# Chunk attention and a mixture of experts on one core: the values' copy behind the next scores, narrower first products, and other orders at the joints

## The chip, the cores and the metric

The kernel runs on one core of a Trainium2 chip, in one launch. The metric is the device time of that core in microseconds (us); the median of several runs is given. The engines are TensorE (PE for matmuls, PEld for their weight loads), VectorE (DVE), ScalarE (ACT), GpSimd (POOL) and SyncE (SP), from whose queue all transfers are issued. PSUM is the memory that TensorE writes its results to; a bank of it holds 128 x 512 float32 numbers.

## The reference

Attention within chunks of 64 tokens, then a mixture of four experts over all 4608 tokens (model width 512, hidden width 1024), all in float32:

```python
scores = scale * q_c @ k_c.T            # 8 batches x 8 heads, chunks of 64 x 64
attn = softmax(scores)
x = (attn @ v_c)                        # then reshaped to (4608, 512)
p = domain_probs / (domain_probs.sum(-1) + 1e-9)
for e in range(4):
    out += p[:, e] * (relu(x @ w1[e]) @ w2[e])
```

## The kernel before

Tokens come in tiles of 128 and in blocks of 512 (four tiles). Block 0 is worked on first and alone, the eight others in four pairs (pairs 0 to 3). A pass is one half (512 columns) of one expert's hidden layer, eight passes for each block or pair.

Every float32 factor is split in a high part (`hi`: a cast on ScalarE) and a low part (`lo`: a subtraction on VectorE or GpSimd), and a product is three matmuls per block of 128 rows (high x high, high x low, low x high; `TERMS`, `PARTS`). `product` issues them all, so nearly all matmuls of the profile have its line (L462). For pairs, the two products of a pass (tokens x w1 and hidden x w2) are done by a scheme with seven block products instead of eight: steps `p1` to `p7` of a group. `g` and `h` are the two groups of the first product, `a` and `b` those of the second; `WOVEN` is the order in which a later pass weaves its `g`, `h` with the `a`, `b` of the pass before. `FIRST` is the order of the first later pass (pair 1, pass 0), which has none before it, and `ALONE` that of the last product, which has none behind. The sums and parts that these steps need (`t1` to `t4` of the tokens in `Tokens`, of the hidden values in `Scaled`) are issued at numbered steps (`add(at, i, ...)`, `put(i, ...)`): the code's order is each engine's order, since the schedule is written by hand (`tc.manual_schedule()`).

Attention for a pair runs beside the passes before, tile by tile: `a_scores` (32 records of small matmuls), `a_softmax`, `a_weights`, `a_transpose`, `a_values`. All of them share the two PSUM banks `psa`: scores lie in the first half of each bank (`blocks(0)`), values in the second (`blocks(1)`). Waits are set by bank: an instruction that touches a bank waits for the other engines' earlier instructions on it. `a_next` issues a tile's values, the copy of the values to SBUF (L176), and then the next tile's scores (L140).

The start does the four tiles of block 0: loads on SP in the order of `load_all`, scores, softmax, transposes, values (`start_...`), then the products x w1 of tiles 0 and 1 together (`plain_hidden`, 256 columns), the output products of tile 0 and 1 (`o[0].whole()`, `o[1].whole()`), and tiles 2 and 3. `keep_warm` issues bf16 matmuls on zeros. A joint is the place where the last pass of a pair goes over into the first of the next: the next pair's tokens are split there (`Tokens`).

Of the kernel before, what the change touches and what calls it, by code (L numbers as in the profile page):

```python
# [8 lines left out]
F32 = mybir.dt.float32  # L9
# [15 lines left out]
WAITS = {"loads": 10, "softmax": 14, "copy": 3}  # L25
# [5 lines left out]
def chunk_attention_moe(ctx: ExitStack, tc: tile.TileContext, qk, v, v0, dp, w1, w2, out):  # L31
# [64 lines left out]
    def transpose_probs():  # L96
        flat = by_e[0].rearrange("p e t -> p (e t)")
        for i in range(0, p_rows, P):
            n = min(P, p_rows - i)
            ps = bank()[:n, :P]  # L100
            rows = hpool.tile([P, P], F32, name="s3")[:n]
# [62 lines left out]
    def a_values(t):  # L164

        s = st.pop(t)
        av = blocks(1)
        for j, rows, c, half, odd in quarters():
            nc.tensor.matmul(  # L169
                av[half, c, j], lhsT=s["v"][rows, 2 * j + odd], rhs=s["pt"][rows, j, half],  # L170
                start=True, stop=True,
            )
# [3 lines left out]
        nc.scalar.copy(  # L176
            out=xraw[pair][:, :, i * P : (i + 1) * P].rearrange("p j (c q) -> p c j q", c=2), in_=av
        )
# [407 lines left out]
    class Scaled:  # L586
# [20 lines left out]
        def __init__(self, n):  # L607
            e = n % n_pass // 2
            self.pb = [(pb[0][:, 0], pb[1])[e % 2], pb[0][:, 1]]
            self.parts, self.values = {}, {}  # L610
# [38 lines left out]
    class LaterGroup(Group):  # L649
        def __init__(self, g, left, h, apart):  # L650
            super().__init__(g, left)
            self.h = h
            i = 1 - g if apart else 0
            self.names = (f"A{i}", f"B{i}", f"C{i}", f"B{i}", "s2")
# [157 lines left out]
    def start_v(t):  # L812
        nc.sync.dma_start(out=v0s[t // GT], in_=v0[:, t : t + GT])

    def start_scores(t):

        sc[t] = bank(("A0", "A1", "C0", "C1")[t]).rearrange("p (h s) -> p h s", s=C)
        for h in range(2 * HG):
            for c in range(2):
                rows = slice(c * C, (c + 1) * C)  # L820
                nc.tensor.matmul(
                    sc[t][rows, h],
                    lhsT=qk0[t][rows, h // HG, 0, h % HG],
                    rhs=qk0[t][rows, h // HG, 1, h % HG],
                    start=True, stop=True,
                )

    def start_transpose(t):

        w = bank(("B0", "B0", "B1", "B0")[t]).rearrange("p (j s) -> p j s", s=P)  # L830
        for j in range(HG):
            nc.tensor.transpose(
                w[:, j], es[t][:, 2 * j : 2 * j + 2].rearrange("p h s -> p (h s)"), ident
            )
        pt[t] = hpool.tile([P, HG, P], F32, name=("s2", "s4")[t % 2])
        nc.scalar.copy(out=pt[t], in_=w)

    def start_values(t):
        av[t] = bank(("B1", "A0", "A1", "B1")[t]).rearrange("p (j s) -> p j s", s=P)
        for j in range(HG):  # L840
            for c in range(2):
                for half in range(2):
                    rows = slice(half * C, (half + 1) * C)
                    cols = slice(c * C, (c + 1) * C)
                    nc.tensor.matmul(
                        av[t][rows, j, cols], lhsT=v0s[t // GT][rows, t % GT, c, j], rhs=pt[t][rows, j, cols],
                        start=True, stop=True,
                    )

    def start_x(t):  # L850
        x_parts(av[t], slice(t * P, (t + 1) * P))
# [6 lines left out]
    idle = bank("C1")  # L858
# [8 lines left out]
    def load_all():  # L867
        start_load(0, 1)
        start_load(1, 2)
        start_v(0)  # L870
        w_loads(0, 0)
        start_load(2, 2)
        start_load(3, 2)
        start_v(2)
        nc.sync.dma_start(out=pr, in_=dp)
# [3 lines left out]
    def start_softmax(t):  # L879
        less_max(sc[t])  # L880
        a_exp(sc[t])

    def start_weights(t):
        es[t] = att.tile([P, 2 * HG, C], F32, name=("e", "pt")[t % 2])
        a_norm(es[t], sc[t], psa[:, 1, t * 2 * HG : (t + 1) * 2 * HG])

    def startup(beside):
# [5 lines left out]
        start_scores(0)  # L893
        start_scores(1)
        keep_warm(WAITS["softmax"])
        start_softmax(0)
        start_softmax(1)
        start_weights(0)
        for f, k in QUADS[:3]:
            w1_split(f, k, nc.gpsimd)  # L900
        start_transpose(0)
        keep_warm(WAITS["copy"])
        start_weights(1)
        start_values(0)
# [12 lines left out]
        start_softmax(3)  # L917
        start_weights(2)
        plain_hidden(0, first, order=RHS_LO_LAST, name="B0")
        w2_split(0, 1)  # L920
        plain_hidden(1, first, order=RHS_LO_LAST, name="B1")
        w2_split(1, 0)
        plain_hidden(2, first, order=RHS_LO_LAST, name="A0")
        start_weights(3)
        start_transpose(2)
        w2_split(1, 1)
        plain_hidden(3, first, order=RHS_LO_LAST, name="C0")
        start_values(2)
        start_x(2)
        norm_probs()  # L930
        o = tiles(0, 0, range(NT), ("A0", "C0", None, None))
# [3 lines left out]
        start_x(3)  # L935
# [3 lines left out]
        for f in range(NK):  # L939
            plain_hidden(f, [2, 3], alloc=False)  # L940
# [167 lines left out]
    def probs_load(n, s):  # L1108
        if not pb:
            pb.append(wpool.tile([P, PAIR, SUB], F32, name="ws"))  # L1110
            pb.append(hpool.tile([P, SUB], F32, name="s4"))
        e = n % n_pass // 2
        t = pb[1] if s == 0 and e % 2 else pb[0][:, s]
# [34 lines left out]
    FIRST = "g1 g2 g6 g5 h1 g7 h2 h6 g4 g3 h5 h7 h4 h3".split()  # L1148

    def first_later_pass(n, *_):  # L1150
# [9 lines left out]
        put(6, "b22", 0)  # L1160
        put(7, "b11", 1)
        put(9, "b21", 0)
        add(at, 9, lambda: sc.sum("t3", 0), lambda: sc.sum("t2", 0))
        put(11, "t2", 0)
        add(at, 11, lambda: sc.sum("t1", 0))
        put(12, "b22", 1)
        put(13, "b21", 1)
        put(13, "t1", 0)
        put(13, "t3", 0)
        add(at, 13, lambda: sc.sum("t4", 0, nc.gpsimd))  # L1170
        add(at, 13, lambda: sc.sum("t1", 1), lambda: sc.sum("t3", 1))
        for i, name in enumerate(FIRST):
# [3 lines left out]
        return (sc, left), []  # L1176

    def later_pass(n, ahead, late):
# [10 lines left out]

        for i, f in late:  # L1190
            add(at, i, f)
        second_half(at, ahead[0])
# [26 lines left out]
        if last_pass and more:  # L1219
# [10 lines left out]
            late = [  # L1230
                (0, lambda: x.hi("b22")), (0, lambda: first_load(pair + 2)), (5, lambda: x.lo("t4")),
                (8, lambda: x.lo("b22")),
# [5 lines left out]
        return (sc, left), late  # L1238

    def second_half(at, sc):  # L1240
# [3 lines left out]
        add(at, 1, lambda: sc.hi("t4", 0), lambda: sc.lo("t4", 0))  # L1244
# [3 lines left out]
        add(at, 6, lambda: sc.hi("t4", 1), lambda: sc.lo("t4", 1))  # L1248

    def last_products(ahead):  # L1250
# [5 lines left out]
        stages += [(wpool, "wraw", N_RAW)] * 3 + [(att, "e", 1), (att, "pt", 1)]  # L1256

        def plane(s, m, ps, engs):
# [4 lines left out]
            pool, name, bufs = stages.pop()  # L1263
            stage = pool.tile([P, NT, P], F32, name=name, bufs=bufs)
            for k, eng in enumerate(engs):
                part = slice(k * NT // len(engs), (k + 1) * NT // len(engs))
                eng(out=stage[:, part], in_=ps[:, part])
            t = (1 + pair * PAIR + s) * NT
            nc.sync.dma_start(
                out=out[t * P : (t + NT) * P, m * P : (m + 1) * P].rearrange("(i p) d -> p i d", p=P),  # L1270
                in_=stage,
            )

        act, dve = [nc.scalar.copy], [nc.vector.tensor_copy]
        for i, name in enumerate(ALONE):
# [3 lines left out]
            if name == "b2":  # L1279
# [8 lines left out]
        plane(0, 3, bank("A1"), act + dve)  # L1288

    with tc.manual_schedule():  # L1290
# [9 lines left out]
        ahead, late = None, []  # L1300
        for n in range(2 * n_pass, n_run):
            ahead, late = (later_pass if n > 2 * n_pass else first_later_pass)(n, ahead, late)
        last_products(ahead)
# [45 lines left out]
```

## Time and profile before

| | |
|---|---|
| runs | 1560.19 us median of 3 (1558.61 to 1560.2) |
| profiled execution | 1559.73 us, span 1557.9 us, mean granted clock 0.999 |
| TensorE busy | 1518.0 us, 97% of the span |
| DVE, ACT, POOL busy | 917.6, 572.5, 886.2 us |
| read and written | 244.39 and 68.23 MB, 201 GB/s over the span |

Start times are us from the span's start. In rows of the trace, a bracket holds the idle time of the engine before the instruction and what ended it; `A<-xh,wf` is what is written and what is read, buffer numbers left out; "x12" is a number of like instructions merged in one row.

### The profile page before, as it was taken

What the parts mean: (1) busy time and instruction counts of PE and PEld (TensorE: products, weight loads), DVE (VectorE), ACT (ScalarE), POOL (GpSimd) and SP (SyncE); (2) the same over time, 40 slices, a digit from 0 to 9 for tenths busy, and PEclk for the clock granted to TensorE, in tenths of its full rate; (3) what the DMA queues carried; (4) which work ended last, traced back from release to release, by engine and by line L of the source; (5) the groups of instructions that cost most, each with busy time, mean ns of one, the idle gap of its engine ahead of it and who ended that gap; (6) DMA issues with size and microseconds to landing.
All of it is one profiled execution on the core that took longest, in us unless ns stands there. A gap on an engine that the chain in (4) does not pass through costs nothing.

```text
span 1557.9 us, 23373 instructions
## 1 busy us (share of the span) xinstructions
PE 1518.0 (97%) x8861; PEld 1241.3 (80%) x8861; DVE 917.6 (59%) x1287; ACT 572.5 (37%) x1000; POOL 886.2 (57%) x666
## 2 busy tenths in 40 slices
PE   8999999999999999999999999999999999999998
PEld 6877777878888887787878787878878788888886
DVE  5444454444444466666666874666767855666665
ACT  3332443444433434333333434332333443333332
POOL 2333577776657616555555764554557655555554
PEclk9999999999999999999999999999999999999999
DMA  5344238966766676666665667666656676666664
GB/s 192 122 122 145 92 129 289 314 226 219 246 217 225 216 256 200 212 205 203 208 203 190 203 211 245 210 201 214 206 182 201 189 237 202 197 201 203 197 194 143
DMA packets 167903, 314.16 MB, mean 202 GB/s; under 512 B 14176, under 2 KB 84080, under 8 KB 167792
## 3 DMA queue, kind: packets, MB, share of 16 engines
q1 hardware_dynamic: 167792, 312.68, 62.1%
q8 instruction: 70, 1.15, 0.3%
q14 instruction: 41, 0.34, 0.1%
HBM read 244.39 MB, written 68.23 MB: 201 GB/s over the span
## 4 chain that ended last, share of the span: by engine, by line
PE 89%; DVE 4%; ACT 2%; POOL 2%; DMA 2%; issue 1%; SPq 0%; POOLq 0%; DVEq 0%; ACTq 0%
PE A L462 44%; PE C L462 26%; PE B L462 14%; PE psa L140 1%; ACT xraw L176 1%; PE psa L169 1%; PE psa L160 1%; DVE xl L275 1%; DVE wraw L635 1%; DVE acc L691 1%; ACT hfh L641 1%; POOL wf L275 0%; PE psa L777 0%; DMA w<-wf 0%; DVE wraw L629 0%
## 5 line engine op out<-in xcount | busy, mean ns | idle before, releaser
L644 POOL TENSOR_TENSOR hfl<-wraw,hfh 128x512 fp32r<-128x512 f32 x288 | 387.2, 1364 | 214.3 <-ACT hfh L641 212.0
L462 PE MATMUL A<-xh,wf 128*128 128x512 f32 (+1 forms) x1112 | 380.7, 389 | 1.0 <-ACT s L524 0.7
L462 PE MATMUL A<-hfh,wf 128*128 128x512 f32 x768 | 271.2, 394 | 1.0 <-DVE acc L691 1.0
L641 ACT CAST hfh<-wraw 128x512 fp32r<-128x512 f32 x288 | 174.0, 622 | 222.6 <-POOL wraw L635 76.4
L462 PEld LDWEIGHTS A<-xh,wf 128*128 128x128 f32 x1112 | 207.8, 188 | 45.6 <-ACT s L524 1.7
L524 ACT COPY s<-A 128x512 f32<-128x512 f32 x192 | 112.9, 588 | 333.4 <-PE A L462 329.0
L462 PE MATMUL A<-xl,wf 128*128 128x512 f32 (+1 forms) x556 | 214.7, 387 | 0.0
L462 PE MATMUL C<-xh,wf 128*128 128x512 f32 (+1 forms) x584 | 201.0, 391 | 0.0
L462 PEld LDWEIGHTS A<-hfh,wf 128*128 128x128 f32 x768 | 144.2, 188 | 32.4 <-DVE acc L691 2.5
L691 DVE TENSOR_TENSOR acc<-A,acc 128x512 f32<-128x512 f32 x174 | 119.2, 685 | 86.0 <-PE A L462 85.5
L462 PE MATMUL A<-hfl,wf 128*128 128x512 f32 x384 | 149.7, 390 | 0.0
L275 POOL TENSOR_TENSOR hfl<-wraw,hfh 128x512 fp32r<-128x512 f32 x64 | 85.8, 1368 | 88.5 <-ACT hfh L272 88.5
L462 PE MATMUL C<-hfh,wf 128*128 128x512 f32 x384 | 134.2, 391 | 0.2
L462 PEld LDWEIGHTS C<-xh,wf 128*128 128x128 f32 x584 | 109.1, 188 | 23.0
L462 PE MATMUL B<-xh,wf 128*128 128x512 f32 (+1 forms) x384 | 126.0, 382 | 0.0
L275 POOL TENSOR_TENSOR wf<-wraw,wf 128x512 fp32r<-128x512 f32 x70 | 91.1, 1324 | 60.0 <-ACT wf L272 59.5
L462 PEld LDWEIGHTS A<-xl,wf 128*128 128x128 f32 x556 | 104.3, 188 | 21.1
L635 POOL TENSOR_TENSOR wf<-wraw,wf 128x512 f32<-128x512 f32 x23 | 29.7, 1291 | 158.4 <-DVE wf L629 158.4
L462 PE MATMUL C<-xl,wf 128*128 128x512 f32 (+1 forms) x292 | 112.8, 388 | 0.0
L691 DVE TENSOR_TENSOR acc<-C,acc 128x512 f32<-128x512 f32 x90 | 62.1, 691 | 66.6 <-PE C L462 59.6
L644 POOL TENSOR_TENSOR hfl<-wf,hfh 128x512 fp32r<-128x512 f32 x48 | 71.1, 1482 | 35.5 <-ACT hfh L641 35.5
L462 PEld LDWEIGHTS C<-hfh,wf 128*128 128x128 f32 x384 | 72.1, 188 | 15.9 <-DVE acc L691 1.1
(179 smaller groups left out, 2732.0 us busy)
## 6 DMA issues: line engine op xcount, KB each, us to landing
wf<-w SPq DMA_DIRECT2D x336, 512.0 KB, 3.9
wraw<-in_w SPq DMA_DIRECT2D x128, 256.0 KB, 3.7
w<-wf SPq DMA_DIRECT2D x112, 256.0 KB, 4.2
qk_in<-in_qk SPq DMA_DIRECT2D x32, 512.0 KB, 4.7
v_in<-in_v SPq DMA_DIRECT2D x32, 256.0 KB, 3.6
w<-hfl SPq DMA_DIRECT2D x32, 256.0 KB, 2.4
w<-hfh SPq DMA_DIRECT2D x32, 256.0 KB, 3.0
w<-hfh SPq DMA_DIRECT2D x48, 128.0 KB, 2.6
```

The costliest lines, as they stand in the source:

```text
L140: nc.tensor.matmul(s["sc"][half, c, j], lhsT=s["x"][rows, g, 0, h], rhs=s["x"][rows, g, 1, h], start=True, stop=True,)
L160: nc.tensor.transpose(ps[:, j], s["e"][:, j].rearrange("p c k -> p (c k)"), ident)
L169: nc.tensor.matmul(av[half, c, j], lhsT=s["v"][rows, 2 * j + odd], rhs=s["pt"][rows, j, half], start=True, stop=True,)
L176: nc.scalar.copy(out=xraw[pair][:, :, i * P : (i + 1) * P].rearrange("p j (c q) -> p c j q", c=2), in_=av)
L275: eng.tensor_tensor(out=t[1], in0=src, in1=t[0].bitcast(F32), op=ALU.subtract)
L462: nc.tensor.matmul(out, lhsT=lhs(k, a), rhs=rhs(k, b), start=first and i == 0, stop=last and i == len(parts) - 1, skip_group_check=not (fi ...
L524: nc.scalar.copy(out=t, in_=self.a)
L635: (eng or nc.vector).tensor_tensor(out=self.values[place, k], in0=self.values[a, k], in1=self.values[b, k], op=op)
L641: nc.scalar.copy(out=self.part(name, 0)[:, k], in_=self.values[name, k])
L644: (eng or nc.gpsimd).tensor_tensor(out=self.part(name, 1)[:, k], in0=self.values[name, k], in1=self.part(name, 0)[:, k].bitcast(F32), op=A ...
L691: nc.vector.tensor_tensor(out=acc[key], in0=src, in1=acc[key], op=ALU.add)
```

## The change

Five places change:

1. `a_values` no longer ends in the copy to SBUF; `a_next` issues the copy (`a_copy`) after the next tile's scores.
2. In the start, the products x w1 of tiles 0 and 1 are done for each tile apart, 128 columns wide, with parts of their own (`xs`); the high x parts come first (`start_hidden(..., False)`), the low ones later. SP loads the first tile's values and two blocks of w1 ahead of the second tile's q and k; six warm-up matmuls stand between the scores of tile 0 and 1, three between those and the first transposes. Other banks are used, and the small sums of the softmax (`z`) get a bank instead of a part of `psa`.
3. `FIRST` has another order, its last two steps (`h4`, `h3`) are issued behind `a1` of the next pass, the group `h` keeps its second copy in `s4` instead of `s2`, and the parts of `t3` and the sum `t4` of the first half go to the next pass.
4. In every joint of passes, the parts of the first half's `t4` move from step 1 to 6, those of the second half from 6 to 7. In the joints of pairs, the low parts of the tokens are issued some steps later than the high ones.
5. The last step `b4` is replaced by `by_halves`: two products of 256 columns in banks of their own, each summed, transposed, copied and stored by itself; the partial sum in `a` is added earlier, behind `b7`.

```diff
+    def a_copy(t):
         pair, i = divmod(t - NT, PAIR * NT)
...
@@ a_next
         if after is not None:
             a_scores(after)
+
+        if t is not None:
+            a_copy(t)
+        if after is not None:
             a_load_v(after)
@@ start
+    def start_x(t):
+        xs[t] = [opool.tile([P, NK, P], F32R, name=f"acc{4 + 2 * t + i}") for i in range(2)]
+        hi_part(av[t], xs[t])
+    def start_x_lo(t):
+        lo_part(nc.vector, av[t], xs[t])
...
+    def start_hidden(t, f, lo):
+        if not lo and f % 2 == 0:
+            hidden[t, f // 2] = bank((("A0", "C0"), ("A1", "B0"))[t][f // 2])
+        n = 2 * NK
+        product(
+            hidden[t, f // 2][:, f % 2 * P : (f % 2 + 1) * P], RHS_LO_LAST[n:] if lo else RHS_LO_LAST[:n],
+            lambda k, a: w1t[f // 2, k // 2][a][:, f % 2, k % 2],
+            lambda k, b: xs[t][b][:, k],
+            first=not lo, last=lo,
+        )
@@ load_all
         start_load(0, 1)
+        start_v(0)
+        w_load(0, 0, 0, 0)
+        w_load(0, 0, 0, 1)
         start_load(1, 2)
-        start_v(0)
-        w_loads(0, 0)
+        w_load(0, 0, 1, 0)
+        w_load(0, 0, 1, 1)
+        start_v(1)
@@ first_later_pass
-    FIRST = "g1 g2 g6 g5 h1 g7 h2 h6 g4 g3 h5 h7 h4 h3".split()
+    FIRST = "g1 g2 g6 g5 g7 h1 h2 g3 g4 h6 h5 h7 h4 h3".split()
...
+        todo = [lambda i=i, name=name: step(i, name) for i, name in enumerate(FIRST)]
+        for f in todo[:-2]:
+            f()
+        return (sc, left), late, todo[-2:]
@@ later_pass, joint of pairs
-            add(at, 15, lambda: x.hi("b11"), lambda: x.lo("b11"))
-            add(at, 16, lambda: x.hi("b21"), lambda: x.lo("b21"))
-            add(at, 18, x.sum4_apart)
-            add(at, 20, x.split2)
-            add(at, 23, lambda: x.hi("t1"), lambda: x.lo("t1"))
-            add(at, 25, lambda: x.hi("t3"), lambda: x.lo("t3"))
+            add(at, 15, lambda: x.hi("b11"))
+            add(at, 16, lambda: x.hi("b21"), lambda: x.lo("b11"))
+            add(at, 17, lambda: x.lo("b21"))
+            add(at, 19, x.sum4_apart)
+            add(at, 21, x.split2)
+            add(at, 23, lambda: x.hi("t1"))
+            add(at, 25, lambda: x.hi("t3"))
             add(at, 26, lambda: x.hi("t4"))
+            add(at, 27, lambda: x.lo("t1"))
@@ last_products
+        def by_halves(o):
+            left, n = o.left(1, "a22", o.g), SUB // 2
+            sums = []
+            for i, ps in enumerate((psa[:, 1], bank("A0"))):
+                cols = slice(i * n, (i + 1) * n)
+                product(ps[:, :n], PARTS, lambda k, a: left[a][:, k], lambda k, b: o.h.part("t4", b)[:, k, cols])
...
+            if name == "b7":
+                steps["b"].add(steps["b"].a, 1, 0)
```

On TensorE, beside a pass of block 0, a tile's values (`pt`, `v_in`) and the next tile's scores (`qk_in`) stood in this order before; in brackets are the queues that a row waits for:

```order
L462 MATMUL C_848<-hfh_768,hfl_808 128x512 [waits DVE_49]
L169 MATMUL psa<-pt,v_in 64x64 [waits DMAHW1_49,Activation_49]
L169 MATMUL psa<-pt,v_in 64x64 x15
L140 MATMUL psa<-qk_in 64x64 [waits DMAHW2_49,Activation_49]
L140 MATMUL psa<-qk_in 64x64 x15
```

The same place after the change:

```order
L468 MATMUL C_906<-hfh_826,hfl_866 128x512 [waits DVE_49]
L169 MATMUL psa<-pt,v_in 64x64 [waits DMAHW3_49,Activation_49]
L169 MATMUL psa<-pt,v_in 64x64 x15
L140 MATMUL psa<-qk_in 64x64 [waits DMAHW4_49]
L140 MATMUL psa<-qk_in 64x64 x15
```

The rows stand as they stood, but the scores no longer wait for ScalarE.

On TensorE in the start, before, from the scores of tile 2 (`xraw`) on: values of tile 1 (`s`, `qk_in`), scores of tile 3, then the first two groups of products of tiles 0 and 1 together (`xh` and `xl` are the parts of x, `wf` those of w1):

```order
L821 MATMUL C_363<-xraw 64x64 x16
L845 MATMUL A_383<-s_361,qk_in 64x64 x16
L821 MATMUL C_402<-xraw 64x64 x16
L462 MATMUL B_443<-xh_236,wf_312 128x256 x4
L462 MATMUL B_443<-xh_236,wf_315 128x256 x4
L462 MATMUL B_443<-xl_237,wf_312 128x256 x2
L462 MATMUL B_443<-xl_237,wf_315 128x256 x2
L462 MATMUL B_462<-xh_236,wf_312 128x256 x4
```

After, from the first product behind the values of tile 0 on (`acc` are now the parts of x; `ident`, `pt` is the transpose of tile 1's weights):

```order
L468 MATMUL A_362<-acc_348,wf_279 128x128 x4
L468 MATMUL A_362<-acc_348,wf_282 128x128 x4
L468 MATMUL C_371<-acc_348,wf_285 128x128 x4
L468 MATMUL C_371<-acc_348,wf_288 128x128 x4
L838 MATMUL B_380<-ident,pt 128x128 x4
L827 MATMUL C_387<-xraw 64x64 x16
L851 MATMUL B_407<-s_385,qk_in 64x64 x16
L468 MATMUL A_362<-acc_349,wf_279 128x128 x2
L468 MATMUL A_362<-acc_349,wf_282 128x128 x2
```

Products of tile 0 now stand ahead of the transposes, scores and values of the next tiles, half as wide and twice as many.

On VectorE in the joint of pairs 1 and 2, before (`xl` is a low part of the tokens, `acc` a sum that empties a PSUM bank of the second product):

```order
L629 SCALAR_TENSOR_TENSOR wraw<-B_8312,ws 128x512
L275 TENSOR_TENSOR xl_8323<-qk_in,xh_8322 128x1024
L691 TENSOR_TENSOR acc_5961<-B_8326,acc_5961 128x512
L691 TENSOR_TENSOR acc_6125<-A_8214,acc_6125 128x512
L275 TENSOR_TENSOR xl_8350<-xraw,xh_8349 128x1024
L629 SCALAR_TENSOR_TENSOR wraw<-A_8189,s_5486 128x512
```

After:

```order
L635 SCALAR_TENSOR_TENSOR wraw<-B_8370,ws 128x512
L697 TENSOR_TENSOR acc_6019<-B_8383,acc_6019 128x512
L697 TENSOR_TENSOR acc_6183<-A_8271,acc_6183 128x512
L635 SCALAR_TENSOR_TENSOR wraw<-A_8247,s_5963 128x512
L670 TENSOR_TENSOR C_8335<-C_8335,s_8306 128x512
L635 SCALAR_TENSOR_TENSOR wf_8236<-C_8335,ws 128x512
```

The two low parts left this stretch; the first of them now stands three rows below these, behind two sums of hidden values.

More of the change, by code (lines that the diff above doesn't have):

```diff
@@ L23 @@
 HF = 512
-WAITS = {"loads": 10, "softmax": 14, "copy": 3}
+WAITS = {"loads": 10, "scores": 6, "softmax": 3, "copy": 3}
 PAIR = 2
@@ L100, in transpose_probs @@
             ps = bank()[:n, :P]
-            rows = hpool.tile([P, P], F32, name="s3")[:n]
+            rows = hpool.tile([P, P], F32, name=("s3", "s4")[i // P % 2])[:n]
             nc.tensor.transpose(ps, flat[:, i : i + n], ident)
@@ L812, in start_v @@
     def start_v(t):
-        nc.sync.dma_start(out=v0s[t // GT], in_=v0[:, t : t + GT])
+        nc.sync.dma_start(out=v0s[t // GT][:, t % GT], in_=v0[:, t])
     def start_scores(t):
-        sc[t] = bank(("A0", "A1", "C0", "C1")[t]).rearrange("p (h s) -> p h s", s=C)
+        sc[t] = (psa[:, 0] if t == 3 else bank(("A0", "A1", "C1")[t])).rearrange("p (h s) -> p h s", s=C)
         for h in range(2 * HG):
@@ L848, in start_values, with start_x_keep, start_relu @@
                     )
+    xs, hidden = {}, {}
     def start_x(t):
-        x_parts(av[t], slice(t * P, (t + 1) * P))
+        xs[t] = [opool.tile([P, NK, P], F32R, name=f"acc{4 + 2 * t + i}") for i in range(2)]
+        hi_part(av[t], xs[t])
+    def start_x_lo(t):
+        lo_part(nc.vector, av[t], xs[t])
+    def start_x_keep(t):
+        for part, one in zip(xt["plain"], xs[t]):
+            nc.scalar.copy(out=part[:, :, t * P : (t + 1) * P], in_=one.bitcast(F32))
+    def start_hidden(t, f, lo):
[8 more added lines that the diff above has]
+        )
+    def start_relu(t):
+        if t == 0:
+            for f in range(NK):
+                h_alloc(0, f)
+        for i in range(2):
+            relu_parts(
+                hidden[t, i][:, : 2 * P].rearrange("p (f c) -> p f c", c=P),
+                *(part[:, :, t * P : (t + 1) * P] for part in hs[0, i]),
+            )
     n_run = n_pass * (1 + n_pairs)
@@ L857, in chunk_attention_moe @@
     nc.vector.memset(zeros, 0.0)
-    idle = bank("C1")
+    idle = psa[:, 0]
     def keep_warm(n, cols=SUB):
@@ L1108, in probs_load @@
     def probs_load(n, s):
-        if not pb:
-            pb.append(wpool.tile([P, PAIR, SUB], F32, name="ws"))
-            pb.append(hpool.tile([P, SUB], F32, name="s4"))
         e = n % n_pass // 2
-        t = pb[1] if s == 0 and e % 2 else pb[0][:, s]
+        i = int(s == 0 and e % 2)
+        if len(pb) == i:
+            pb.append((hpool.tile([P, SUB], F32, name="s4") if i else wpool.tile([P, PAIR, SUB], F32, name="ws")))
+        t = pb[1] if i else pb[0][:, s]
         r = e * n_tiles + (1 + (n // n_pass - 1) * PAIR + s) * NT
@@ L1188, in put @@
             add(at, i, lambda: of.hi(name, k), lambda: of.lo(name, k))
+        for f in held:
+            add(at, 0, f)
+        second_half(at, ahead[0])
         for i, f in late:
             add(at, i, f)
-        second_half(at, ahead[0])
         add(at, 12, lambda: sc.sum("t3", 0, nc.gpsimd))
@@ L1237, in later_pass @@
                 f()
-        return (sc, left), late
+        return (sc, left), late, ()
     def second_half(at, sc):
@@ L1255, in last_products, with store, plane @@
         stages = [(hpool, f"s{i}", 1) for i in (1, 2, 3)]
-        stages += [(wpool, "wraw", N_RAW)] * 3 + [(att, "e", 1), (att, "pt", 1)]
-        def plane(s, m, ps, engs):
+        stages += [(wpool, "wraw", N_RAW)] * 4 + [(att, "e", 1), (att, "pt", 1)]
+        def store(s, m, ps, eng, rows=range(NT)):
+            pool, name, bufs = stages.pop()
+            stage = pool.tile([P, len(rows), P], F32, name=name, bufs=bufs)
+            eng(out=stage, in_=ps)
+            t = (1 + pair * PAIR + s) * NT + rows[0]
+            nc.sync.dma_start(
+                out=out[t * P : (t + len(rows)) * P, m * P : (m + 1) * P].rearrange("(i p) d -> p i d", p=P),
+                in_=stage,
+            )
+        def plane(s, m, ps, eng):
             ps = ps.rearrange("p (i d) -> p i d", d=P)
@@ L1262, in plane @@
                 output_part(pair, s * NT + j, m, ps[:, j])
[L1263 to L1275, printed above, removed]
+            store(s, m, ps, eng)
+        def by_halves(o):
[4 more added lines that the diff above has]
+                product(ps[:, :n], PARTS, lambda k, a: left[a][:, k], lambda k, b: o.h.part("t4", b)[:, k, cols])
+                sums.append(opool.tile([P, n], F32, name=f"acc{NK + i}"))
+                nc.vector.tensor_tensor(
+                    out=sums[i], in0=ps[:, :n], in1=acc[o.n // n_pass, 2 + o.g][:, cols], op=ALU.add
+                )
+            for i, ps in enumerate((bank("A1"), bank("B1"))):
+                ps = ps[:, :n].rearrange("p (i d) -> p i d", d=P)
+                for j in range(n // P):
+                    nc.tensor.transpose(ps[:, j], sums[i][:, j * P : (j + 1) * P], ident)
+                store(0, 2 + o.g, ps, (nc.scalar.copy, nc.vector.tensor_copy)[i], range(2 * i, 2 * i + 2))
+        act, dve = nc.scalar.copy, nc.vector.tensor_copy
+        for i, name in enumerate(ALONE[:-1]):
             getattr(steps[name[0]], f"p{name[1]}")()
```

121 lines of the change are left out of this document (70 added, 51 removed).

## The prediction

> **What bounds the kernel now.** I read the page's shares first, then the stretches by time, the list of waits for TensorE (PE, and PEld for its weight loads), and last the timelines of the places that these name.
>
> ```profile
> PE 1518.0 (97%) x8861; PEld 1241.3 (80%) x8861; DVE 917.6 (59%) x1287; ACT 572.5 (37%) x1000; POOL 886.2 (57%) x666
> ```
>
> TensorE is the bound. The next rows give start:end, length, its busy time, granted clock, DMA share and GB/s: what it still loses lies before 28.71 us, around 600 us, and in the last 9 us. Where no attention runs beside it (1240 to 1520), it loses nothing.
>
> ```profile
> 0.00:28.71 28.71, 24.75 (x314) 0.94 0.75 247
> 28.71:47.38 18.67, 18.67 (x162) 1.00 0.18 52
> 600.00:612.00 12.00, 10.74 (x47) 1.00 0.52 162
> 1240.00:1520.00 280.00, 280.00 (x1252) 1.00 0.64 204
> 1549.00:1558.00 9.00, 3.98 (x28) 0.99 0.77 219
> ```
>
> The list of waits (waiter, line, releaser: us in total, times, longest) says what the rest is; one entry is larger than all others together.
>
> ```profile
> PEld psa L140 <- ACT xraw L176: 29.6, 28, 1.7
> PE psa L140 <- ACT xraw L176: 25.8, 28, 1.6
> PE C L462 <- POOL hfl L644: 1.5, 2, 1.3
> PE B L832 <- DVE hfl L470: 1.1, 1, 1.1
> PE A L462 <- DVE acc L691: 1.0, 2, 0.5
> PE psa L140 <- DMA qk_in<-in_qk: 0.4, 1, 0.4
> ```
>
> **Values copied behind the scores.** One of the 28 sites (start, length, then idle time before in brackets):
>
> ```profile
> 61.86 0.69 PE L169 MATMUL psa<-pt,v_in 64*64 64x64 f32 x32
> 61.87 0.54 PEld L169 LDWEIGHTS psa<-pt,v_in 64*64 64x64 f32 x30
> 62.62 0.59 ACT L176 COPY xraw<-psa 128x512 f32<-128x512 f32 x1 [1.23 <-PE psa L169]
> 63.26 0.56 PEld L140 LDWEIGHTS psa<-qk_in 64*64 64x64 f32 x32 [0.84 <-ACT xraw L176]
> ```
>
> The scores do not use what the copy reads. They share its two PSUM banks, so before they wait for ScalarE (ACT) to begin and end a 0.59 us copy. After the change the order shows no ScalarE wait ahead of these scores. The gain lies between PE's 25.8 us and PEld's 29.6. A PE end is modelled and covers part of each stall, while the next weight load can follow the last one directly, so I take PEld's, less 0.3 for seams: **-29.3 us**. The copy then starts about 0.6 us later, behind 32 more matmuls. Queued behind it on ScalarE are casts and the next tile's exp; VectorE's (DVE) row maximum of the next tile waits for the copy too. Their cover is one TensorE step of several us; without it one 0.59 us copy per site, 28 x 0.6 = 17 us, would return. SP's loads of the next values and of the next q and k stand behind the same matmuls as before, which now end sooner: no cost.
>
> **The start.** Twelve products per tile and block of w1, each 128 columns wide (96 in all), replace 48 of 256 columns.
>
> ```profile
> 8.03 1.88 PE L821 MATMUL A<-xraw 64*64 64x64 f32 x32 [1.69 <-DMA xraw<-in_qk]
> 15.00 1.15 PE L845 MATMUL B<-s,qk_in 64*64 64x64 f32 x32
> 17.64 1.10 PE L845 MATMUL A<-s,qk_in 64*64 64x64 f32 x32
> 18.58 1.10 PE L821 MATMUL C<-xraw 64*64 64x64 f32 x32
> 21.02 1.03 PEld L462 LDWEIGHTS B<-xh,wf 128*128 128x128 f32 x8
> 22.46 1.03 PEld L462 LDWEIGHTS A<-xh,wf 128*128 128x128 f32 x8
> 25.24 0.65 PE L832 MATMUL B<-ident,e 128*128 128x128 f32 x4 [1.06 <-DVE hfl L470]
> 28.74 0.48 PE L462 MATMUL A<-hfh,hfh 128*128 128x512 f32 x1
> 4.77:8.18 3.41, 1.73 (x39) 1.00 0.89 275
> 8.18:11.60 3.42, 3.42 (x37) 0.50 1.01 344
> ```
>
> Two groups of twelve 256-column products start 1.44 us apart (21.02, 22.46): 0.120 us each, 48 x 0.120 = 5.8 us. What a 128-column product costs, no row shows. Half of 0.120 is one end (0.06: 96 cost 5.8, no loss). The other is the 0.227 us of a 512-column product (1536.57 to 1536.80 below). I take 0.120, the row with the same 128x128 weight load, which width doesn't shorten: 96 x 0.120 = 11.5, **+5.8** over before. From the first values (15.00) to the first output product (28.74) before spends 13.74 us. It loses the 1.2 us stall at 25.24 and gains three warm-up matmuls (0.7): 13.7 + 5.8 - 1.2 + 0.7 = 19.0.
>
> When do the first values start? The second tile's q and k now stand behind 0.25 MB of values and 0.5 MB of weights in SP's queue. They landed at 8.03 before; 0.75 MB more at 344 GB/s is 2.2 us, so 10.2. Its scores stand ahead of the first transposes on TensorE. Behind them follow 0.98 us of scores at full clock (17.64 to 18.58 is 0.94) or 1.88 at half, warm-up, transposes and a 0.6 us copy: values at 13.3 at full clock, 15.0 at half. I take the middle, 14.2: six warm-up matmuls now stand in the gap that lowered the clock (0.50 in the last row), but they end by 8.8 and leave another. The output product then starts at 14.2 + 19.0 = 33.2, against 28.74: **+4.5 us**, between -2.2 (0.06 each, values at 13.3) and +15.6 (0.227 each, values at 15.0). From 28.71 on, TensorE was dense and does the same work, so nothing absorbs it. The smaller edits there (z in a bank of its own, four ScalarE copies of x parts, relu by pairs) stand under those products: no cost, or 0.6 us apiece where a product waits for one.
>
> The Trainium skill has a lower price in its page TensorE: Matmul & The Clock Gate (Back-to-back issue gap), about 81 ns sustained for 128 columns; by it 96 cost 7.8 us and the sum is 3.7 us lower, but it also gives 131 ns for 512 columns, where this trace has 227. The same page (Part 1) lets the clock fall after an idle window of some 3.4 us; by it the gap, now split over two windows, would leave full clock and a sum 0.9 us lower, but here the clock fell after a window in which TensorE was busy 1.73 of 3.41 us.
>
> **First later pass.** Two waits of the list stand here, one for a copy and one for GpSimd (POOL):
>
> ```profile
> 590.38 0.59 ACT L524 COPY s<-A 128x512 f32<-128x512 f32 x1 [0.78 <-PE A L462]
> 591.02 0.50 PE L462 MATMUL A<-xh,wf 128*128 128x512 f32 x1 [0.73 <-ACT s L524]
> 599.98 1.74 POOL L635 TENSOR_TENSOR wraw<-wraw 128x512 f32<-128x512 f32 x1
> 601.68 2.51 POOL L644 TENSOR_TENSOR hfl<-wraw,hfh 128x512 fp32r<-128x512 f32 x2
> ```
>
> A separate buffer and a1 in front of h4 take the 0.7 us wait for the copy. The 1.74 us sum and t3's low part go behind t1's low part on POOL, for which a5 waits 1.3 us. In exchange h3 ends one product (1.36 us) nearer to a5, and g1 now follows h3 into the bank that h4's relu must empty. I take **-1.6** of the 2.0, between -2.0 and 0. In the other passes t4's low parts only move behind t2's and t3's, and a4 reads them six products later: nothing.
>
> **The joints** of pairs 1 and 2, and 2 and 3:
>
> ```profile
> 872.85 1.38 DVE L275 TENSOR_TENSOR xl<-xraw,xh 128x1024 fp32r<-128x1024 f32 x1 [0.25 <-ACT xh L272]
> 884.04 1.48 DVE L275 TENSOR_TENSOR xl<-qk_in,xh 128x1024 fp32r<-128x1024 f32 x1 [0.30 <-ACT xh L272]
> 886.05 0.68 DVE L691 TENSOR_TENSOR acc<-A,acc 128x512 f32<-128x512 f32 x1
> 886.78 0.50 PE L462 MATMUL A<-hfh,wf 128*128 128x512 f32 x1 [0.53 <-DVE acc L691]
> ```
>
> The long low parts of the tokens stand ahead of the sums that empty PSUM. Put behind them they free some 0.5 us at the first and the second place of a joint: 2 x 0.95 = **-1.9**; 0 at least.
>
> **The last product.**
>
> ```profile
> 1536.57 0.39 PE L462 MATMUL A<-hfh,wf 128*128 128x512 f32 x1
> 1536.80 0.39 PE L462 MATMUL A<-hfl,wf 128*128 128x512 f32 x1
> 1550.69 0.48 PE L462 MATMUL A<-hfh,wf 128*128 128x512 f32 x1
> 1552.36 0.69 DVE L691 TENSOR_TENSOR acc<-A,acc 128x512 f32<-128x512 f32 x1 [1.14 <-PE A L462]
> 1553.80 0.37 ACT L1267 COPY s<-A 128x256 f32<-128x256 f32 x1 [2.25 <-PE A L777]
> 1554.21 0.42 DVE L1267 COPY s<-A 128x256 f32<-128x256 f32 x1 [1.15 <-ACT s L1267]
> ```
>
> By halves, 12 x 0.12 = 1.44 us replace 6 x 0.227 = 1.36 (+0.1). The last sum has half the width (0.42 for 0.69), two transposes of four and the 0.4 us between the two copies leave the chain: -0.3 - 0.3 - 0.4, and the DMA that ends last carries half the bytes (-0.3). With 0.3 for a6, which waited behind t4's low part on POOL, **-1.5**, between -2.0 and 0. The earlier sum of `b7` lies under five planes.
>
> **Sum.** -29.3 + 4.5 - 1.6 - 1.9 - 1.5 = -29.8. The profiled execution took 1559.73 (its span and 1.83 around it), so it goes to 1529.9; it lies 0.46 below the median of the runs, so the median goes to **1530.4 us**.
>
> **Rivals.**
> - *The wait moves on.* The copy's later end holds casts on ScalarE, and half of the 29.3 us returns: 1545. Against it: apart from the copy the list has only some 5 us of waits on engines. Chance 0.08.
> - *Narrow products cost as much as 512-column ones* (0.227): 1530.4 + 10.3 = 1540.7. No row excludes it. 0.10.
> - *They cost half of a 256-column one* (0.06): 1530.4 - 5.8 = 1524.6. Against it stands the full weight load. 0.08. (The page's 81 ns gives 1526.7, between this and the forecast.)
> - *The scores find another late thing at the old place* (the 0.4 us wait for `qk_in` stands there once): the 29.3 us stay, 1559.7. 0.03.
> - *Slower:* a denser TensorE is granted less clock. 1% is 15 us; from 2.0% (29.9 / 1518) on nothing is won, at 2.5% it is 1530.4 + 38 = 1568. Against it: 280 us at 100% busy ran at 1.00. 0.03.
>
> The forecast, 1522 to 1537, has 0.68. The range 1522 to 1541 takes in both narrow-product cases and leaves out the rest. A change of 0.2% (3 us) is about what a measurement can tell from none: faster 0.95, same 0.02, slower 0.03.
>
> **What the profile after would show.** The list of waits without ScalarE's copy ahead of the scores (right), or with another entry of 10 us or more under casts (first rival). The first output product at 31 to 35 us, and groups of 128-column products at 0.11 to 0.12 us each; at 0.06 or 0.23 the start is mis-sized. No wait above 0.5 us near the first later pass and the two joints; the last copy ends within 3.0 us of the last product's start (3.9 now, 1550.69 to 1554.63). The prediction is wrong if the start costs over 10 us or a granted clock below 0.99 appears.

## The result, and the profile after

The changed kernel takes 1530.94 us (median of 6 runs, 1530.01 to 1532.5) against 1559.05 for the kernel before beside it: ratio 0.982 (95% interval 0.9807 to 0.9832). Run again in a later set it gave 0.9811 (0.9798 to 0.9824). The forecast was 1530.4. The sum came out, but not all its terms: one had the wrong sign, one was nothing.

The page of the changed kernel, and its list of waits for TensorE (us in total, times, longest):

```profile
PE 1516.4 (99%) x8912; PEld 1246.3 (81%) x8913; DVE 921.3 (60%) x1289; ACT 574.7 (38%) x1004; POOL 874.9 (57%) x666
```

```profile
PE A L468 <- DVE acc L697: 3.8, 2, 1.9
PE A L827 <- DMA xraw<-in_qk: 2.4, 1, 2.4
PE psa L903 <- DVE s L897: 1.2, 1, 1.2
PE psa L140 <- DMA qk_in<-in_qk: 0.8, 1, 0.8
PE C L468 <- DVE hfl L476: 0.7, 1, 0.7
PE C L468 <- POOL hfl L650: 0.3, 1, 0.3
```

The 28 waits for ScalarE's copy are gone, and no other entry under a cast took their place. New at the top stands a sum on VectorE, twice 1.9 us: these are the two joints. A site of the copy (timeline, TensorE and ScalarE):

```profile
65.79 0.69 PE L169 MATMUL psa<-pt,v_in 64*64 64x64 f32 x32
66.31 0.65 PE L140 MATMUL psa<-qk_in 64*64 64x64 f32 x32
67.02 0.59 ACT L178 COPY xraw<-psa 128x512 f32<-128x512 f32 x1 [1.70 <-PE psa L140]
```

From the values' start to the scores' start it was 1.40 us (61.86 to 63.26), now it is 0.52; to the first product behind the scores it was 2.03 (to 63.89), now it is 1.10 (to 66.89). The stretches that answer to those shown of before, and the joint (start:end, length, TensorE busy, granted clock, DMA share, GB/s):

```profile
0.00:32.65 32.65, 28.75 (x360) 0.95 0.67 222
600.00:612.00 12.00, 12.00 (x85) 1.00 0.82 259
858.00:862.00 4.00, 2.11 (x7) 0.83 0.57 187
862.00:866.00 4.00, 4.00 (x15) 0.75 0.42 131
```

The first later pass, 10.74 of 12 us busy before, is full. In the joint at 858 TensorE is busy for half of the time, and then runs at a lower clock. The start and the joint on TensorE:

```profile
9.68 1.15 PE L827 MATMUL A<-xraw 64*64 64x64 f32 x32 [2.38 <-DMA xraw<-in_qk]
14.23 1.15 PE L851 MATMUL B<-s,qk_in 64*64 64x64 f32 x32
20.47 2.00 PE L468 MATMUL A<-acc,wf 128*128 128x128 f32 x16
22.31 1.95 PE L468 MATMUL C<-acc,wf 128*128 128x128 f32 x16
32.67 0.48 PE L468 MATMUL C<-hfh,hfh 128*128 128x512 f32 x1
858.02 0.39 PE L468 MATMUL B<-hfh,wf 128*128 128x512 f32 x1
860.30 0.55 PE L468 MATMUL A<-hfh,wf 128*128 128x512 f32 x1 [1.89 <-DVE acc L697]
```

Stalls below are counted from start to start, less the 0.227 us of one product: 858.02 to 860.30 is 2.05.

### The profile page after: what moved, and what is told of

Read it like the earlier page. It is cut to its first block, busy times and chain, and to the rows that moved or that the text cites. A ratio compares the mean times of both kernels' runs of the same rounds, so it can differ in the third digit from the quotient of the medians.

```text
span 1530.7 us, 23497 instructions
## 1 busy us (share of the span) xinstructions
PE 1516.4 (99%) x8912; PEld 1246.3 (81%) x8913; DVE 921.3 (60%) x1289; ACT 574.7 (38%) x1004; POOL 874.9 (57%) x666
## 3 DMA queue, kind: packets, MB, share of 16 engines
q8 instruction: 70, 1.15, 0.3%
## 4 chain that ended last, share of the span: by engine, by line
PE 95%; DVE 2%; issue 1%; DMA 1%; POOL 1%; SPq 0%; ACT 0%; POOLq 0%; DVEq 0%; ACTq 0%
PE A L468 47%; PE C L468 27%; PE B L468 16%; PE psa L169 1%; DVE xl L281 1%; PE psa L140 1%; PE psa L160 1%; PE psa L783 0%; DMA xraw<-in_qk 0%; DVE acc L697 0%; POOL hfl L281 0%; DMA qk_in<-in_qk 0%; DVE xraw L438 0%; PE psa L903 0%; DVE wraw L641 0%
## 5 line engine op out<-in xcount | busy, mean ns | idle before, releaser
L650 POOL TENSOR_TENSOR hfl<-wraw,hfh 128x512 fp32r<-128x512 f32 x288 | 377.7, 1326 | 226.1 <-ACT hfh L647 223.7
L468 PE MATMUL A<-hfh,wf 128*128 128x512 f32 (+1 forms) x768 | 271.9, 396 | 3.8 <-DVE acc L697 3.8
L281 POOL TENSOR_TENSOR hfl<-wraw,hfh 128x512 fp32r<-128x512 f32 x64 | 84.9, 1353 | 92.8 <-ACT hfh L278 90.9
```

What stands on the lines that cost most here:

```text
L281: eng.tensor_tensor(out=t[1], in0=src, in1=t[0].bitcast(F32), op=ALU.subtract)
L468: nc.tensor.matmul(out, lhsT=lhs(k, a), rhs=rhs(k, b), start=first and i == 0, stop=last and i == len(parts) - 1, skip_group_check=not (fi ...
L650: (eng or nc.gpsimd).tensor_tensor(out=self.part(name, 1)[:, k], in0=self.values[name, k], in1=self.part(name, 0)[:, k].bitcast(F32), op=A ...
```

## The experiments

Each was timed beside the kernel before, whose median was 1560.26 us in the first set of four, 1559.6 in the second, 1559.39 in the third.

**Part 1 alone.**

```diff
 (kernel before)
-        nc.scalar.copy(...)        # end of a_values
+        if t is not None:          # a_next, behind a_scores
+            a_copy(t)
...
```

> The kernel before with part 1 alone (the values' copy behind the next tile's scores). Theory: the 28 waits of the scores vanish and nothing takes their place, 29 to 31 us less than before, so 1528 to 1530. Rival: the later copy holds casts on ScalarE and the shorter passes let other waits grow, and half of it returns: about 1544.

Measured: 1527.39, ratio 0.9788 (0.9775 to 0.9801), 32.9 us less (29 to 31 were expected). Part 1 alone is 0.2 to 0.3% faster than all five together. The reverse, the changed kernel with part 1 undone:

> The changed kernel with its first part alone undone: the copy of the values stands ahead of the next tile's scores again. Theory: the 28 waits of the scores for ScalarE's copy are back, 29.3 us, and the time is about 1560 us, ratio 0.999 to 1.001 to the kernel before, since the other four parts together give nothing or lose 1 to 2 us. Rival: part of the wait goes elsewhere in the changed kernel, and undoing it costs less than 26 us (below 1557).

Measured: 1562.2, ratio 1.0015 (1.0006 to 1.0024), 32.0 us more than the changed kernel beside it. The waits are back in its list, the same 25.8 us by TensorE's modelled ends:

```profile
PE psa L140 <- ACT xraw L176: 25.8, 28, 1.6
```

So the other four parts together lose 2.8 us (1562.2 against 1559.39; 0 to 2 were expected).

**The start as before.**

```diff
-    (products of tiles 0 and 1 apart, 128 wide; values and w1 loaded ahead of tile 1)
+    (start of the kernel before: 256 wide, its loads, banks and warm-up)
```

> The changed kernel with the start of before (loads, warm-up, products of tiles 0 and 1 together). Theory: twice as many products at the same price each delay the first output product by 3.9 us (32.67 against 28.74) and all behind it: 3.9 us less than the changed kernel, about 1527. Rival: the later part waits for loads or GpSimd anyway and takes the gain back: 1531.

Measured: 1527.0, ratio 0.9788 (0.9775 to 0.9801). Its first output product, the row that answers to 32.67 above:

```profile
27.43 0.48 PE L468 MATMUL A<-hfh,hfh 128*128 128x512 f32 x1
```

**The first later pass as before.** (The old `FIRST` with all its steps in its own pass, one buffer `s2`, the sums and parts at their old steps.)

```diff
-    FIRST = "g1 g2 g6 g5 g7 h1 h2 g3 g4 h6 h5 h7 h4 h3".split()
+    FIRST = "g1 g2 g6 g5 h1 g7 h2 h6 g4 g3 h5 h7 h4 h3".split()
...
```

> The changed kernel with the first later pass in the order of before and one buffer for the kept copies. Theory: the three stalls of before (0.27, 0.89 and 1.42 us) come back: 2.6 us more than the changed kernel, about 1533.5. Rival: they hung on the timing of the attention beside them and stay away: 1531.

Measured: 1533.14, ratio 0.9827 (0.9814 to 0.984), 1 to 2.5 us above the changed kernel's two ratios, which the intervals alone can't tell from none. Three stalls stand in its trace again, 0.26, 0.89 and 1.43 us; the changed kernel has none there.

**The joints of pairs as before.** (All the steps that the diff moves there.)

```diff
-            add(at, 19, x.sum4_apart)
-            add(at, 21, x.split2)
+            add(at, 18, x.sum4_apart)
+            add(at, 20, x.split2)
...
```

> The changed kernel with the orders at the joint of two pairs as before. Theory: the new order itself makes the 2.05 us stall at each of the two joints and the 1.6 us at half clock behind it; with the old order the stalls of before (1.2 us a joint) come back instead: 2 x (2.05 + 1.6 - 1.2) = 5 us less than the changed kernel, about 1526. Rival: the passes, shortened by the copy's move, shift VectorE against GpSimd, and the stall comes in the old order too: 1531, as the changed kernel.

Measured: 1527.15, ratio 0.9792 (0.9778 to 0.9805). The stalls of 2.05 us are gone, the old ones are back (0.35, 0.66 and 0.24 us in each joint). The steps that part 4 moves in the joints of pairs thus made these joints worse; its other half, the parts of `t4` in every joint of passes, was not undone by itself. VectorE in the changed kernel, and GpSimd beside it:

```profile
848.16 2.36 DVE L281 TENSOR_TENSOR xl<-xraw,xh 128x1024 fp32r<-128x1024 f32 x1
851.04 1.72 DVE L281 TENSOR_TENSOR xl<-xraw,xh 128x1024 fp32r<-128x1024 f32 x1
854.48 1.78 DVE L438 TENSOR_TENSOR xraw<-xraw,pt 128x512 f32<-128x512 f32 x1
856.18 0.68 DVE L697 TENSOR_TENSOR acc<-C,acc 128x512 f32<-128x512 f32 x1
856.78 1.18 DVE L281 TENSOR_TENSOR xl<-e,xh 128x512 fp32r<-128x512 f32 x1
857.89 1.75 DVE L281 TENSOR_TENSOR xl<-pt,xh 128x512 fp32r<-128x512 f32 x1
859.57 0.68 DVE L697 TENSOR_TENSOR acc<-A,acc 128x512 f32<-128x512 f32 x1
854.14 3.27 POOL L650 TENSOR_TENSOR hfl<-wraw,hfh 128x512 fp32r<-128x512 f32 x2 [2.47 <-ACT hfh L647]
857.38 1.72 POOL L650 TENSOR_TENSOR hfl<-wf,hfh 128x512 fp32r<-128x512 f32 x1
```

TensorE waits for the last of the VectorE rows (859.57). The three rows of `xraw` and `xl` closest ahead of it read SBUF twice and take 1.2 to 1.8 us; the sums in between, of the same size, with one input in PSUM, take 0.68. In the kernel before, the two of 128x1024 took 1.22 and 1.38 (870.78, 872.85), and these three:

```profile
876.46 0.68 DVE L432 TENSOR_TENSOR xraw<-xraw,pt 128x512 f32<-128x512 f32 x1
878.45 1.65 DVE L275 TENSOR_TENSOR xl<-e,xh 128x512 fp32r<-128x512 f32 x1
880.02 0.68 DVE L275 TENSOR_TENSOR xl<-pt,xh 128x512 fp32r<-128x512 f32 x1
```

Is it the sums' step or the late low parts? Two runs undo one edit each, a third undoes both:

```diff
 joint_sums
-            add(at, 19, x.sum4_apart)
-            add(at, 21, x.split2)
+            add(at, 18, x.sum4_apart)
+            add(at, 20, x.split2)
 joint_lows
-            add(at, 15, lambda: x.hi("b11"))
-            add(at, 16, lambda: x.hi("b21"), lambda: x.lo("b11"))
-            add(at, 17, lambda: x.lo("b21"))
+            add(at, 15, lambda: x.hi("b11"), lambda: x.lo("b11"))
+            add(at, 16, lambda: x.hi("b21"), lambda: x.lo("b21"))
```

> The changed kernel, but in the two joints of pairs the sums of t4 and the split of t2 (sum4_apart, split2: six VectorE operations that read SBUF twice) stand one step earlier, at 18 and 20, where they stood before the change; all the low parts stay late. Theory A (place of the sums): the stall of 2.05 us at 858 and 1185 of the changed kernel comes from these six operations running beside GpSimd's subtractions, in which the row xraw took 1.78 us, xl<-e 1.18 and xl<-pt 1.75 instead of 0.68. One step (six products, 1.36 us) earlier they run ahead of that burst; the stall falls below 0.7 us in each joint and the ratio to the kernel before goes from 0.982 to 0.979 or 0.980 (about 1527 us). Theory B (late low parts): b11's and b21's low parts, put in front of these sums' queue later, are what makes VectorE late; then the stall stays at about 2 us less one operation (1.4 us or more) and the ratio stays at 0.981 to 0.982.

> The changed kernel, but in the two joints of pairs the low parts of b11 and b21 stand directly behind their high parts again (steps 15 and 16); the sums of t4 and the split of t2 stay at 19 and 21. Theory A (place of the sums): the stall of about 2 us stays, 1.5 to 2.1 us per joint, and the ratio stays at 0.981 to 0.982. Theory B (late low parts): the stall falls below 0.7 us and the ratio is 0.979 to 0.980 (about 1527 us).

> The changed kernel with both of these edits of the joints of pairs undone (low parts of b11 and b21 directly behind the high ones, sums at 18 and 20); only the low parts of t1 and t3 stay late. Theory A expects the stall of 2.05 us gone and the old 0.66 and 0.24 us per joint gone with it, so that only about 0.35 us per joint is left: 2 to 3 us below the changed kernel's undisturbed joints, ratio 0.978 to 0.979 (about 1526 us). Rival: late t1 and t3 parts bring a stall of their own behind the sums; then it is no better than the order before the change (0.979 to 0.980) or worse.

Measured: ratios 0.9802 (0.9788 to 0.9815), 0.9798 (0.9784 to 0.9811) and, with both undone, 0.9787 (0.9774 to 0.98). Neither theory held for the single edits: each halves the stall, to 1.15 and 1.18 us with the sums back, to 1.07 and 1.05 with the low parts back. Each leaves three of the five long operations long: 2.36, 1.71 and 1.63 us with the sums back, 1.78, 1.18 and 1.78 with the low parts back.

With both undone the 2.05 us are gone, and so are the old 0.66 and 0.24; about 0.35 us are left there, and 0.53 and 0.22 us a little later, where a low part of GpSimd is late. Against the old order the late parts of `t1` and `t3` bring at most about a us (0.9787 against 0.9792, inside the intervals).

What makes VectorE late is then asked with its order untouched:

```diff
+            lo = of.lo
+            if last_pass and more and 16 <= i <= 22:
+                lo = lambda name, k: nc.gpsimd.memset(of.part(name, 1)[:, k].bitcast(F32), 0.0)
-            add(at, i, lambda: of.hi(name, k), lambda: of.lo(name, k))
+            add(at, i, lambda: of.hi(name, k), lambda: lo(name, k))
```

> The changed kernel with the order of its joints untouched, but in the last passes of pairs 1 and 2 GpSimd's low parts of steps 16 to 22 (b11 twice, t2, b22, t3: five subtractions of 128x512) are not computed; a fill with zeros of the same size stands in their place, which reads no SBUF. This leaves out the low parts of those hidden values. Theory C (the two engines hold each other up where both read SBUF): VectorE's operations there fall back to 0.68 us for 128x512 and about 1.22 us for 128x1024 (they took 1.18 to 1.78 and 1.72 to 2.36), and the stall of 2.05 us falls below 0.3 us with no other change on VectorE; ratio 0.979 to 0.980. Rival D (VectorE has simply too many operations in front of the sum that TensorE waits for, whatever GpSimd does): the lengths stay within 0.2 us of the changed kernel's and the stall stays above 1.5 us; ratio 0.981 to 0.982.

Measured: 1523.32, ratio 0.9769 (0.9756 to 0.9782). The rows that answer to those above:

```profile
852.01 0.69 DVE L438 TENSOR_TENSOR xraw<-xraw,pt 128x512 f32<-128x512 f32 x1
853.24 0.69 DVE L281 TENSOR_TENSOR xl<-e,xh 128x512 fp32r<-128x512 f32 x1
853.85 0.68 DVE L281 TENSOR_TENSOR xl<-pt,xh 128x512 fp32r<-128x512 f32 x1
854.79 0.69 DVE L697 TENSOR_TENSOR acc<-A,acc 128x512 f32<-128x512 f32 x1 [0.25 <-PE A L468]
851.86 0.53 POOL L1258 MEMSET hfl<- 128x512 f32 x1 [0.83 <-PE C L468]
854.58 0.53 POOL L1258 MEMSET hfl<- 128x512 f32 x1 [2.19 <-PE A L468]
```

All three lengthened operations fell to 0.68 or 0.69 us, the sum now waits for TensorE instead of the reverse, and no stall above 0.15 us is left in either joint. Theory C is shown, and D is out: the two engines hold each other up. (The ratio is lower than expected; with the stall, the stretches at half clock and the wait for GpSimd's late low part are gone from the trace too.) A fill is also shorter (0.53 for 1.3 us), but what the three VectorE operations read from GpSimd (`e`, `pt`) was done some 10 us earlier, so that shortens none of them.

**The last product as before**, beside the changed kernel itself:

```diff
-        by_halves(steps["b"])
+        plane(0, 3, bank("A1"), act + dve)
...
```

> The changed kernel with its last product as before: one step b4 of 512 columns, one sum, four transposes, two copies one behind the other, and the partial sum in a added at its old place. The prediction gave the new last product 1.5 us (between 0 and 2.0), of which 0.3 belong to a wait elsewhere that did not go. Theory: 1.0 to 1.3 us slower than the changed kernel run beside it, with 3.9 us from the last product's start to the end of the last copy against about 3.0. Rival: the transfer of the last output sets the end, and the halves save nothing: within 0.3 us.

> The changed kernel itself, beside the others of this set, as the base for differences of one or two us: ratio to the kernel before 0.982, about 1531 us. In the executions seen so far the 2.05 us stall in the two joints of pairs was followed by a stretch at half clock in one trace and by none in two variants; the trace of this run shows whether the stretch belongs to the kernel or to the execution. If to the kernel, both joints show matmuls 0.43 us apart again, if to the execution, one or both do not.

Measured: 1530.51 with the old last product, ratio 0.9813 (0.98 to 0.9827); 1530.17 for the changed kernel. No difference: the rival was right. First and last rows of the end, of the changed kernel and then of this one:

```profile
1523.45 0.36 PE L468 MATMUL psa<-hfh,wf 128*128 128x256 f32 x1
1526.11 0.42 DVE L1334 COPY s<-B 128x256 f32<-128x256 f32 x1 [0.53 <-PE B L1361]
```

```profile
1521.82 0.48 PE L468 MATMUL A<-hfh,wf 128*128 128x512 f32 x1
1525.35 0.42 DVE L1339 COPY s<-A 128x256 f32<-128x256 f32 x1 [1.16 <-ACT s L1339]
```

The last copy ends 3.08 instead of 3.95 us behind the product's start, but the span ends 7.25 (1530.7) and 7.38 us (1529.2) behind it, and 7.21 in the kernel before. The stretches of the changed kernel's end (the five engines' busy time, clock, DMA share, GB/s) say why:

```profile
1523.45:1526.60 3.15, 2.40 (x19) 1.86 (x17) 1.91 (x4) 1.01 (x3) 0.00 (x0) 1.00 0.98 275
1526.60:1528.90 2.30, 0.00 (x0) 0.00 (x0) 0.00 (x0) 0.00 (x0) 0.00 (x0) 1.00 1.02 287
```

From the last product's start until 2.3 us after every engine is done the transfers run at full share. SP issued these from 1522.65 on (KB each, median us from issue to landing):

```profile
out<-wraw SPq DMA_DIRECT2D x4, 256.0 KB, 3.1
out<-s SPq DMA_DIRECT2D x1, 256.0 KB, 4.0
out<-s SPq DMA_DIRECT2D x2, 128.0 KB, 3.2
```

That is 1.5 MB, or 5.5 us at 287 GB/s, and 1523.45 to 1528.90 is 5.45: the queue of outputs sets the end, not the last chain.

The chain to the last copy is 0.87 us shorter, and the last store takes that back. Before, it was issued 0.03 us behind the last copy's end (1554.66) and landed after 2.3 us; now it is issued 0.34 us behind (1526.87) and lands after 2.9 us, with half the bytes (the kernel before, then the changed one):

```profile
out<-s SPq DMA_DIRECT2D x1, 256.0 KB, 2.3
```

```profile
out<-s SPq DMA_DIRECT2D x1, 128.0 KB, 2.9
```

**The clock in the joints.** Of 12 stalls of 2.05 us or more (two each in six traces), six were followed by some 3.4 us of products 0.427 us apart instead of 0.227, six by none; of the changed kernel's own two traces, both joints in the first, only the second joint in the other. The traces show what decides. By the clock records of each trace, the granted clock changes only at whole multiples of 3.413 us: in the changed kernel's first trace it falls at 10.70, 860.61 and 1188.29, which lie 249 and 96 times 3.413 us apart. Cut at these multiples, the stretch of a stall and the one behind it, and then the stretch of the first stall (856.21 to 858.52) of the second trace (start:end, length, TensorE busy, clock, DMA share, GB/s):

```profile
857.20:860.61 3.41, 1.52 (x7) 1.00 0.84 278
860.61:864.02 3.41, 3.41 (x9) 0.50 0.05 16
```

```profile
854.75:858.16 3.41, 1.85 (x9) 1.00 0.85 258
```

The first stall lies in one such stretch; the other crosses an end, and the next 3.41 us ran at full clock. In all six cases with half clock TensorE was busy for 1.49 to 1.52 us of the stretch before; in the six without, it was busy for 1.56 to 2.37 us of the emptier stretch. The busy time alone is no general limit (at the start, matmuls of 64x64 busy for 1.73 us were followed by half clock too), but here it tells all twelve apart. Around the four stalls of 1.05 to 1.18 us each stretch was busy for 2.4 us or more, and none was followed by half clock.

So the code's order makes a stall long enough, and where it falls in the 3.413 us, which differs from execution to execution, decides on the half clock. A stretch at half clock costs 1.4 to 1.6 us. Where none follows, TensorE waits 0.54 and 0.22 us some 15 us later, where a low part of GpSimd is late, so that the difference between the two cases is below a us.

**The best of both**: the changed kernel with the start of before and the two edits of joint_first.

> The changed kernel with the start of the kernel before and with the low parts of b11 and b21 and the sums of the tokens at their old steps (15, 16, 18, 20). Theory: the two gains add, since the places lie 820 us apart: 5.2 us in the start (output product at 27.4 instead of 32.7) and 4.6 us in the joints, so 1521 to 1522 us, ratio 0.975 to 0.976, and below both kernels. Rival: the earlier start is lost in later waits for loads of the first passes, and only the joints' 4.6 us are left: 1526 us, 0.979.

Measured: 1523.81, ratio 0.977 (0.9757 to 0.9783), 6.4 us below the changed kernel beside it, 2 to 3 above the forecast; the rival (1526) is out. On top of joint_first (0.9787) the old start brings 2.4 us by the ratios and 3.3 by the spans of the two traces (1525.0 and 1521.7), not 5.2. The 5.2 was the distance between two single executions, one at half clock in the start and one not (see the start below).

## Why the prediction was right, point by point

| term | predicted | measured | from |
|---|---|---|---|
| copy | -29.3 | -32.1 | 28 sites, values' start to the first product behind the scores; -32.0 and -32.9 in the runs |
| start | +4.5 | +3.9 | output product at 32.67, was 28.74 |
| first later pass | -1.6 | -2.6 | 0.27, 0.89 and 1.42 us gone |
| joints | -1.9 | +4.7 | 2 x 2.05 and 15 products 0.2 us slower, was 2 x 1.21; +3.3 where no half clock follows |
| last product | -1.5 | 0.0 | 7.21 to 7.25 us from its start to the end |

The measured terms add up to -26.1, against -27.2 between the two spans (1557.9 and 1530.7); 1.1 us are not assigned to a place. The mechanism of the largest term was right, and with it the size of the whole. That the median came within 0.5 us of the forecast was luck: joints and last product were 8.1 us worse than forecast, copy, pass and start 4.4 us better, the profiled span fell by 2.6 us less than forecast, and the profiled execution (1532.5) was the slowest of the six.

- *Copy: right, 2.8 us too small.* The mechanism, the sites and the cover on ScalarE were as said. Mis-sized was the choice of PEld's 29.6 less seams. From the first matmul of the values to the first product behind the scores, the 28 sites took 62.7 us before and 30.6 after. Of the 32.1 us, 30.8 lie ahead of the scores (at the site shown 1.40 less 0.52 is 0.88, where the lists have 0.84 and 0.70) and 1.3 within them.
- *Start: right, in part by luck.* From the values to the output product it took 18.44 us (19.0 forecast): 18.44 to 18.75 in all ten traces with the new start, 13.74 to 13.76 in the four with the old. The narrow products cost (22.31 - 20.47) / 16 = 0.115 us each, beside 0.120 for twice the width. The 81 ns that the Trainium skill's page TensorE: Matmul & The Clock Gate gives (Back-to-back issue gap) don't hold here. The values started at 14.23 (14.2 forecast), but 14.2 was the middle between two clocks, and it was met by an execution at half clock (0.62 from 9.70 to 14.20). Of the ten, two ran so (values at 14.20 and 14.23), eight at full clock (12.06 to 13.46). The output product came at 30.5 to 32.95 (mean 31.5), with the old start at 27.4 to 29.2 (mean 28.3); at a like clock the new start costs 3.6 to 3.9 us. The products lose 4.7 us and the earlier values gain about 1 us back; what the width alone costs was not tried.
- *First later pass: right, 1.0 too small.* 0.3 come from reading stalls by modelled ends, 0.3 are a stall that the prediction didn't count, and the 0.4 that it took off for `h3` and `g1` did not come.
- *Joints: wrong, by 6.6 us (5.2 where no half clock follows).* The failed step is "Put behind them they free some 0.5 us": VectorE's operations were moved at the lengths that they had at their old place. One step (1.36 us) later they met GpSimd's subtractions, and five of them, 0.68 or 1.22 us long by themselves, took 4.3 us longer together (2.36, 1.72, 1.78, 1.18 and 1.75). "No wait above 0.5 us" was the line that the profile contradicts.
- *Last product: wrong.* The chain to the last copy shortened by 0.9 us, as forecast (3.08; 3.0 was named). The failed step is that "the DMA that ends last carries half the bytes (-0.3)": in the full queue it was issued 0.3 us later and took 0.6 longer. The wait of `a6` for GpSimd (0.3) stayed as well.
- *The rivals.* No wait moved on under ScalarE's casts. Narrow products at 0.06 or 0.227 are both out. The mean clock was 0.996 (0.999 before); what it lost beside the start (0.95 there) lies mostly in the two stretches behind a stall, not in dense work.

## What to carry to other kernels

When an instruction is moved on an engine, don't carry its length along: look at what GpSimd does at the new place, and count a VectorE operation with two SBUF inputs at up to its own time plus the rest of GpSimd's subtraction (1.75 for 0.68 at 857.89). Size a gap of TensorE from start to start, and an end from the last byte: where transfers ran at full share past the last copy, a shorter chain of copies bought nothing. Time the parts alone as well, since here the first alone was faster than all five.

## What was not expected of the hardware

A VectorE operation with both inputs in SBUF and a GpSimd subtraction hold each other up, and when both begin at nearly the same time either can be the one that waits. The same two instructions in the kernel before, and with part 1 alone (DVE, then GpSimd):

```profile
886.65 1.21 DVE L275 TENSOR_TENSOR xl<-xraw,xh 128x1024 fp32r<-128x1024 f32 x1
886.63 2.37 POOL L644 TENSOR_TENSOR hfl<-wraw,hfh 128x512 fp32r<-128x512 f32 x1
```

```profile
863.54 2.35 DVE L281 TENSOR_TENSOR xl<-xraw,xh 128x1024 fp32r<-128x1024 f32 x1
863.53 1.28 POOL L650 TENSOR_TENSOR hfl<-wraw,hfh 128x512 fp32r<-128x512 f32 x1
```

The code's order is the same, and GpSimd begins 0.01 to 0.02 us ahead in both. In the first GpSimd takes 1.1 us more than undisturbed (1.3) and VectorE nothing; in the second VectorE pays 1.14 and GpSimd nothing, and TensorE's stall there grows from 0.24 to 1.39. The Trainium skill has the rule in SBUF — State Buffer (Who interferes with whom): a VectorE instruction with two SBUF inputs contends with a GpSimd instruction that reads SBUF, and the one issued second waits for the other to end. The traces agree where the starts lie apart (854.48, behind GpSimd's of 854.14, took 1.78 instead of 0.68); sums with an input in PSUM stay at 0.68, and beside a fill, which reads nothing, nothing is lengthened. For starts as close as these two, the recorded times don't tell who was first.

The clock's grid of 3.413 us was not expected either. The Trainium skill's page TensorE: Matmul & The Clock Gate (Part 1) says that the clock is set by activity in a free-running window of some 3.4 us. The traces agree: within a trace all its changes lie on one grid, and the grid lies elsewhere in each execution (a stretch begins at 857.20 in one trace of the changed kernel and at 854.75 in the other). That a window with TensorE busy for 1.52 of 3.41 us is enough for half clock is what these traces add.
